# Attention beside linear attention on one core: part of the exponentials moved to VectorE, 32-row score tiles, and a listed order

## The chip, the cores and the metric

The kernel runs on one core of a Trainium2 chip. A core has TensorE (PE; its weight loads appear as PEld), ScalarE (ACT), VectorE (DVE), GpSimd (POOL) and SyncE (SP), which run side by side, each in its own program order, and wait for each other on semaphores. DMA queues move data between HBM and the on-chip memory SBUF. Matrix products land in PSUM, eight banks of 128 partitions x 512 fp32. The metric is the device time of one execution in microseconds (us), lower is better.

## The reference

Two attention blocks read the same `x` (2048 tokens, width 512, bf16), each with 32 heads of 16; a per-token gate mixes them.

```python
g = sigmoid((x * gate_w).sum(-1, keepdims=True))
# A: softmax attention
q, k, v = split_heads(x @ A_wqkv)                  # 32 heads of 16
p = softmax(q @ k.T * 16 ** -0.5)                  # 2048 x 2048 for each head
a = merge_heads(p @ v) @ A_wo
# B: linear attention
q, k, v = split_heads(x @ B_wqkv)
pq, pk = phi(q), phi(k)                            # phi(t) = t+1 if t>0 else exp(t), plus 1e-6
b = merge_heads((pq @ (pk.T @ v)) / (pq @ pk.sum() + 1e-6)) @ B_wo
out = g * a + (1 - g) * b
```

Block A needs 32 x 2048 x 2048 exponentials: 134 million, 1.05 million on each of the 128 partitions. A unit here is one head, 128 keys and 512 queries: a tile of 128 x 512 exponentials. There are 32 x 16 x 4 = 2048 units.

## The kernel before

Softmax is computed without subtracting a maximum; the row sum comes from a column of ones beside V, so one product gives numerator and denominator. The work goes in 32 rounds: four blocks `t8` of eight heads, two halves of four heads, four chunks `qc` of 512 queries. A round has 64 units (16 key blocks x 4 heads), cut into 22 groups (`sizes`, line 695: twenty of three units and two of two).

For each group the loop at the end of the function calls, in this order:

- `emit_ST` (line 710): one score matmul for each unit, 128 keys x 512 queries. A head has only 16 rows, but the stationary operand `KTpad` has all 128: `task_KPAD` (line 418) masks K with `maskK`, so that the seven other heads' rows are zeros. Group g writes banks 0 to 2 or 3 to 5 in turn (`b0 = 3 * (g % 2)`).
- `emit_EXP` (line 726): one ACT instruction over the whole group, 128 x 1536, from PSUM to `PT` in SBUF, which has four slots.
- `emit_PV` (line 734) of the group two before: `PT` is stationary in pieces of 128 x 128 and 32 columns of `Vaug` (16 of V, a one, 15 zeros) stream past it, four matmuls a unit, added up in bank 6 (`acc`).
- at a round's end `emit_round_end` (line 753): DVE takes the reciprocal of the row sums and scales the numerators.

Everything else is cut into steps with deadlines and costs (`enqueue`, `run_misc`): projections of Q, K, V, and block B. `run_misc` fits steps between groups by a credit of PE and DVE time, and none runs in the first two or last three groups of a round (`quiet`, line 926). All these steps share bank 7. Block B takes the exponential of phi from PSUM on ACT (`phi_ops`, line 513) and evicts the tile on DVE after it; `task_BQ` (line 582) takes reciprocals of whole 128 x 512 tiles of denominators in pieces of 128 columns. The first exponentials need a slice of `A_wqkv` (`wA0`), loaded on ACT's DMA queue behind two halves of `x` (`xnat`); the other halves of `x` come by DMA transposes on SP's queue.

Each engine's list is fixed when the program is built, and an engine that waits holds everything behind it. So ACT's step to the next group needs its banks filled, and PE can fill them only after ACT's instruction two groups before has ended.

Of the kernel before, what the change touches and what calls it, by code (L numbers as in the profile page):

```python
# [2 lines left out]

# [8 lines left out]
I32 = mybir.dt.int32  # L12


DEBUG_REQ = lambda env: []
STATS = {}
SCHED_LOG = []
# [18 lines left out]
class _Eng:  # L36
    def __init__(self, name, sem):
        self.name = name
        self.sem = sem
        self.ops = []  # L40
        self.n = 0
        self.inc_idx = []
        self.inc_val = []
        self.semval = 0
        self.waited = {}

# [9 lines left out]
    def add(self, fn, deps=(), inc=True, dma_sem=None):  # L56
        waits = []
        for d in deps:
            if d is None:
                continue  # L60
            if isinstance(d, _Raw):
                sem, val = d.sem, d.val
            else:
                sem, val = d.E.sem, d.E.cover(d.idx)
            key = id(sem)
            if val <= 0 or self.waited.get(key, 0) >= val:
                continue
            self.waited[key] = val
            for k, (s2, v2) in enumerate(waits):
                if s2 is sem:  # L70
                    if val > v2:
                        waits[k] = (sem, val)
                    break
            else:
                waits.append((sem, val))
# [10 lines left out]
class _Res:  # L86
    __slots__ = ("name", "w", "r")

    def __init__(self, name):
        self.name = name  # L90
        self.w = None
        self.r = {}

# [20 lines left out]

def bass_gated_mix__mha_block__linear_attn_block__prompt_kernel(
# [11 lines left out]
    assert Bsz == 1  # L127
    H = 32
    Dh = D // H
    assert Dh == 16 and D % 128 == 0 and S % 512 == 0  # L130
# [5 lines left out]
    NU = NTB * 4  # L136
    GS = 3
    NPT = 4

    with ExitStack() as es:  # L140
# [8 lines left out]

        xT = SB([128, NCC, S], BF16, "xT")  # L150
        NCP = NCC // 2
        xnat = SB([128, NTB, 128 * max(NCP, 1)], BF16, "xnat")
        dummy = SB([128, 2], FP32, "dummy")
        wA = SB([128, NCC, 3 * D], BF16, "wA")
        wA0 = SB([128, NCC, 3, 128], BF16, "wA0")
# [6 lines left out]
        pidx_i = SB([128, 1], I32, "pidxi")  # L162
        hidx_f = SB([128, 1], FP32, "hidxf")
        mtmp = SB([128, 8], FP32, "mtmp")
        maskK = SB([128, 8], FP32, "maskK")
        blockmask = SB([128, 128], BF16, "blockmask")
        KT = SB([128, 1, S], BF16, "KT")
        KTpad = SB([128, 2, 4, S], BF16, "KTpad")
        QT = SB([128, 2, NQC, 512], BF16, "QT")
        Vaug = SB([128, 2, NTB, 4, 32], BF16, "Vaug")  # L170
        PT = SB([128, NPT, 512 * GS], BF16, "PT")
        O_sb = SB([128, NTB, D], BF16, "Osb")
        rden = SB([128, 16], FP32, "rden")
        tpool = SB([128, 2, 512], FP32, "tpool")
        epool = SB([128, 2, 512], FP32, "epool")
        upool = SB([128, 2, 512], FP32, "upool")
        phiK = SB([128, 2, D], BF16, "phiK")
        vB = SB([128, 2, NCC, 136], BF16, "vB")
        kvacc = SB([128, NCC, 136], FP32, "kvacc")
        KVbd = SB([128, NCC, 128], BF16, "KVbd")  # L180
        Zexp = SB([128, NCC, 128], BF16, "Zexp")
        phiQT = SB([128, 2, NCC, 512], BF16, "phiQT")
        numT = SB([128, 2, 512], FP32, "numT")
        den = SB([128, 2, 512], FP32, "den")
        OBT = SB([128, 2, NCC, 512], BF16, "OBT")
        bB = SB([128, NQC, 4, D], BF16, "bB")
        OT = SB([128, 4, NCC, 128], BF16, "OT")
        NOUTT = 2
        outt = SB([128, NOUTT, D], BF16, "outt")
        eg = SB([128, NTB], FP32, "eg")  # L190
        gom = SB([128, 2, NTB], FP32, "gom")

        STATS["sbuf_free"] = nc.sbuf_bytes_remaining() if callable(getattr(nc, "sbuf_bytes_remaining", None)) else nc.sbuf_bytes_remaining
# [3 lines left out]
        spare = ps[:, 3584:4096]  # L197
        spare_bf = ps[:, 3584:4096].bitcast(BF16)
        acc4 = acc.rearrange("p (qb j c) -> p qb j c", qb=4, j=4)

        PE = _Eng("pe", SEM("s_pe"))
# [5 lines left out]
        semXN = [SEM("s_xn0"), SEM("s_xn1")]  # L207
        semW0 = SEM("s_w0")
# [3 lines left out]
        semW3 = SEM("s_w3")  # L212
        semOUT = [SEM(f"s_out{i}") for i in range(NOUTT)]
        out_counts = [0] * NOUTT

        R = _Res
        r_ring = [R(f"ring{b}") for b in range(6)]
        r_acc = R("acc")
        r_spare = R("spare")
        r_xT = [[R(f"xT{c}_{t}") for t in range(NQC)] for c in range(NCC)]  # L220
        r_xnat = [R(f"xnat{i}") for i in range(2)]
        r_wA = R("wA")
        r_wA0 = R("wA0")
        r_warm = R("warm")
        r_wB = R("wB")
        r_woA = R("woA")
        r_woB = R("woB")
        r_gw = R("gw")
        r_ident = R("ident")
        r_const = R("const")  # L230
        r_mask = R("mask")
        r_bmask = R("bmask")
        r_dummy = R("dummy")
        r_KT = [[R(f"KT{p}_{t}") for t in range(NQC)] for p in range(1)]
        r_KTpad = [[[R(f"KTpad{p}_{j}_{t}") for t in range(NQC)] for j in range(4)] for p in range(2)]
        r_QT = [[R(f"QT{p}_{q}") for q in range(NQC)] for p in range(2)]
        NVB = max(1, (NTB + 3) // 4)
        r_Vaug = [[R(f"Vaug{p}_{v}") for v in range(NVB)] for p in range(2)]
        r_Vaug_all = [r for row in r_Vaug for r in row]
        r_PT = [R(f"PT{i}") for i in range(NPT)]  # L240
        r_O = [R(f"O{qb}") for qb in range(NTB)]
        r_rden = R("rden")
        r_t = [R(f"t{i}") for i in range(2)]
        r_e = [R(f"e{i}") for i in range(2)]
        r_u = [R(f"u{i}") for i in range(2)]
        r_phiK = [R("phiK0"), R("phiK1")]
        r_vB = [R("vB0"), R("vB1")]
        r_kvacc = R("kvacc")
        r_KVbd = R("KVbd")
        r_Zexp = R("Zexp")  # L250
        r_phiQT = [[R(f"phiQT{p}_{i}") for i in range(NCC)] for p in range(2)]
        r_numT = [R("numT0"), R("numT1")]
        r_den = [R("den0"), R("den1")]
        r_OBT = [[R(f"OBT{p}_{i}") for i in range(NCC)] for p in range(2)]
        r_bB = [[R(f"bB{q}_{b}") for b in range(4)] for q in range(NQC)]
        r_OT = [R(f"OT{i}") for i in range(4)]
        r_outt = [R(f"outt{i}") for i in range(NOUTT)]
        r_eg = R("eg")
        r_g = R("g")

        def op(E, fn, reads=(), writes=(), inc=True, extra=()):
            deps = _deps_for(reads, writes) + list(extra)
            ev = E.add(fn, deps, inc=inc)
            _record(E, ev, reads, writes)
            return ev

# [8 lines left out]
        def dma(out_ap, in_ap, sem, reads=(), writes=(), total_after=None, noncontig=False, E=None, transpose=False):  # L275
            E = SP if E is None else E
            eng = {SP: nc.sync, AC: nc.scalar, PO: nc.gpsimd}[E] if E in (SP, AC, PO) else nc.sync
            deps = _deps_for(reads, writes)
            ev = E.add(lambda o=out_ap, i=in_ap, nz=noncontig, tr=transpose, eng=eng: _do_dma(eng, o, i, nz, tr),
                       deps, inc=False, dma_sem=sem)  # L280
            for res in reads:
                res.r[E] = _Raw(sem, total_after)
            for res in writes:
                res.w = _Raw(sem, total_after)
                res.r = {}
            return ev

        def pe_macro(fns, reads=(), writes=(), record=True, wait=True):
            assert fns
            deps = _deps_for(reads, writes) if wait else []  # L290
            first = None
            ev = None
            for k, fn in enumerate(fns):
                last = (k == len(fns) - 1)
                ev = PE.add(fn, deps if k == 0 else (), inc=(last and record))
                if k == 0:
                    first = ev
            if record:
                for res in reads:
                    res.r[PE] = first  # L300
                for res in writes:
                    res.w = ev
                    res.r = {}
            return ev

# [5 lines left out]

        x2 = A_x[0]
        out2 = out[0]
        wsrc = A_wqkv.rearrange("(cc p) n -> p cc n", p=128)
        if NCP > 0:
            for hh in range(2):
                dma(xnat[:, hh * (NTB // 2):(hh + 1) * (NTB // 2), :],
                    x2[hh * (S // 2):(hh + 1) * (S // 2), 128 * (NCC - NCP):D].rearrange("(tb p) c -> p tb c", p=128),
                    semXN[hh], writes=[r_xnat[hh]], total_after=16, E=AC)
        for k3 in range(3):  # L320
            dma(wA0[:, :, k3, :], wsrc[:, :, k3 * D:k3 * D + 128], semW0, writes=[], total_after=48, E=AC)
        r_wA0.w = _Raw(semW0, 48)
        dma(gw[:], gate_w.rearrange("(cc p) -> p cc", p=128), semG, writes=[r_gw], total_after=16, noncontig=True, E=AC)
        NCD = NCC - NCP
        for t in range(NQC):
            for cc in range(NCD):
                dma(xT[:, cc, 512 * t:512 * (t + 1)], x2[512 * t:512 * (t + 1), 128 * cc:128 * (cc + 1)], semXT[cc][t],
                    writes=[r_xT[cc][t]], total_after=16, transpose=True, E=SP)
        dma(wA[:], wsrc, semW1, writes=[r_wA], total_after=16)
        dma(wB[:], B_wqkv.rearrange("(cc p) n -> p cc n", p=128), semW2, writes=[r_wB], total_after=16)  # L330
        dma(woA[:], A_wo.rearrange("(i p) n -> p i n", p=128), semW3, writes=[r_woA], total_after=32)
# [710 lines left out]
```

## Time and profile before

| | |
|---|---|
| three runs, median (lowest to highest) | 972.21 us (972.05 to 972.5) |
| the profiled execution's own time: its span | 970.5 us |
| ACT busy | 945.0 us, 97% |
| PE busy | 832.4 us, 86% |
| DVE busy | 305.9 us, 32% |
| first group exponential starts / last one ends | 16.60 us / 961.9 us |
| group exponentials of 1536 and of 1024 columns | 640 and 64 |

The span runs from the first to the last instruction of the one execution that was profiled; the median is 1.7 us above it. Busy shares are averages, and a busy PE includes the pipelined ends of its matmuls. A row of the groups names the line, engine, operation and tiles, and then the busy time of all and the mean of one. Matmul rows have the line of a helper, so they are told apart by their tiles. The chain of waits follows the work that ended last back from the end of the program.

### The profile page before, as it was taken

To read this page: it belongs to the slowest core of one execution; us is meant where nothing else is said; L and a number is where in the kernel's file an instruction comes from. 1 tells how busy PE (TensorE), PEld (TensorE's weight loads), DVE (VectorE), ACT (ScalarE), POOL (GpSimd) and SP (SyncE) were. 2 spreads that over 40 slices of the span, in tenths; PEclk is the share of its full clock that TensorE was granted. 3 is DMA by queue.
4 is the path that set the end of the run, shared out by engine and by line. 5 is a ranking of instruction groups with operands and counts; after the bars stand their busy time and mean duration, and the time that the engine had idled before them with its cause. 6 is when DMAs were issued, how large, how long until landed. Compare 5 with 4: busy or idle time off the path is not lost.

```text
span 970.5 us, 25037 instructions
## 1 busy us (share of the span) xinstructions
PE 832.4 (86%) x11257; PEld 504.8 (52%) x11464; DVE 305.9 (32%) x591; ACT 945.0 (97%) x739; POOL 8.1 (1%) x42
## 2 busy tenths in 40 slices
PE   6988888898888988888888888888888898879886
PEld 3555555555555555555545555554555555545553
DVE  3311132032321223223654445344555431102112
ACT  3999999999999999999999999999999999999996
POOL 3000000000000000000000000000000000000000
PEclk8999999999999999999999999999999999999998
DMA  9000000000000000000000000000000000000001
GB/s 275 3 2 1 2 2 1 2 1 2 2 2 2 2 1 2 1 2 2 2 1 2 2 1 2 2 1 1 1 2 2 1 2 1 1 2 18 12 18 45
DMA packets 13067, 10.40 MB, mean 11 GB/s; under 512 B 6816, under 2 KB 11936, under 8 KB 12960
## 3 DMA queue, kind: packets, MB, share of 16 engines
q1 hardware_dynamic: 8768, 7.34, 2.5%
q10 hardware_dynamic: 4192, 1.44, 0.7%
q8 instruction: 90, 1.47, 0.6%
q14 instruction: 17, 0.14, 0.1%
HBM read 5.64 MB, written 2.10 MB: 8 GB/s over the span
## 4 chain that ended last, share of the span: by engine, by line
ACT 52%; PE 30%; issue 14%; DVE 2%; DMA 1%; ACTq 1%; DVEq 0%
ACT PT L730 51%; PE ps L307 30%; DVE den L613 1%; ACT epool L514 1%; DMA wA_5<-in_A_wqkv_dram 1%; DVE tpool L516 1%; ACTq L273 0%; DVE outt L677 0%; DVE den L607 0%; PE ps L310 0%; DMA out_dram<-outt 0%; DVE KTpad L425 0%; ACTq L992 0%; ACTq L985 0%; DVE KT L413 0%
## 5 line engine op out<-in xcount | busy, mean ns | idle before, releaser
L730 ACT ACTIVATE PT<-ps 128x1536 bf16<-128x1536 f32 (+1 forms) x704 | 934.2, 1465 | 10.6 <-PE ps L307 9.5
L307 PE MATMUL ps<-QT,KTpad 128*128 128x512 bf16 x1883 | 529.4, 381 | 116.6 <-ACT PT L730 108.4
L307 PEld LDWEIGHTS ps<-Vaug,PT 128*128 128x128 bf16 x8192 | 308.0, 96 | 166.7 <-ACT PT L730 0.8
L307 PE MATMUL ps<-Vaug,PT 128*128 128x32 bf16 x8192 | 313.8, 176 | 1.0 <-ACT PT L730 0.4
L307 PEld LDWEIGHTS ps<-QT,KTpad 128*128 128x128 bf16 x2048 | 152.4, 97 | 247.6 <-ACT PT L730 139.9
L756 DVE RECIPROCAL rden<-ps 128x16 f32<-128x16 f32 x32 | 8.2, 257 | 190.8 <-PE ps L307 190.8
L613 DVE RECIPROCAL den<-den 128x128 f32<-128x128 f32 x64 | 61.0, 953 | 2.2
L516 DVE COPY tpool<-ps 128x512 f32<-128x512 f32 x32 | 22.1, 691 | 91.0 <-ACT epool L514 91.0
L465 DVE CAST Vaug<-ps 128x256 bf16<-128x256 f32 x32 | 13.6, 424 | 78.9 <-PE ps L307 78.9
L425 DVE TENSOR_SCALAR KTpad<-KT,maskK 128x512 bf16<-128x512 bf16 x128 | 34.6, 346 | 0.1
L307 PE MATMUL ps<-wB,xT 128*128 128x512 bf16 x116 | 31.1, 377 | 3.1 <-DVE tpool L516 2.6
L564 DVE TENSOR_TENSOR kvacc<-ps,kvacc 128x258 f32<-128x258 f32 x32 | 13.7, 428 | 57.4 <-PE ps L307 57.4
L307 PE MATMUL ps<-xT,wA 128*128 128x512 bf16 x100 | 27.0, 377 | 0.5
L482 DVE CAST QT<-ps 128x512 bf16<-128x512 f32 x16 | 11.1, 691 | 42.4 <-PE ps L307 42.4
L413 DVE CAST KT<-ps 128x512 bf16<-128x512 f32 x16 | 11.1, 692 | 39.4 <-PE ps L307 39.4
L514 ACT ACTIVATE epool<-ps 128x512 f32<-128x512 f32 x32 | 21.8, 682 | 0.0
L677 DVE SCALAR_TENSOR_TENSOR outt<-ps,gom,bB 128x512 bf16<-128x512 f32 x16 | 11.8, 749 | 28.3 <-PE ps L307 26.8
L645 DVE TENSOR_SCALAR bB<-ps,gom 128x512 bf16<-128x512 f32 x16 | 12.0, 750 | 26.6 <-PE ps L307 26.6
L607 DVE TENSOR_SCALAR den<-ps 128x512 f32<-128x512 f32 x16 | 11.1, 691 | 29.6 <-PE ps L307 29.6
L307 PE MATMUL ps<-wA,xT 128*128 128x64 bf16 x448 | 18.7, 192 | 0.0
L307 PE MATMUL ps<-woA,OT 128*128 128x512 bf16 x58 | 16.6, 390 | 0.8 <-DVE OT L667 0.6
L667 DVE COPY OT<-ps 128x512 bf16<-128x512 bf16 (+2 forms) x20 | 7.1, 369 | 30.9 <-PE ps L310 30.9
(61 smaller groups left out, 246.1 us busy)
## 6 DMA issues: line engine op xcount, KB each, us to landing
out_dram<-outt SPq DMA_DIRECT2D x16, 128.0 KB, 1.7
wA<-in_A_wqkv_dram SPq DMA_DIRECT2D x1, 1536.0 KB, 7.0
wB<-in_B_wqkv_dram SPq DMA_DIRECT2D x1, 1536.0 KB, 10.3
xnat<-in_A_x_dram ACTq DMA_DIRECT2D x2, 512.0 KB, 5.3
woA<-in_A_wo_dram SPq DMA_DIRECT2D x1, 512.0 KB, 11.3
woB<-in_B_wo_dram SPq DMA_DIRECT2D x1, 512.0 KB, 12.2
wA_5<-in_A_wqkv_dram ACTq DMA_DIRECT2D x3, 128.0 KB, 6.9
xT<-in_A_x_dram SPq DMA_TRANSPOSE x8, 6.0
```

Of the source, the lines that this page charges most:

```text
L307: return lambda: nc.tensor.matmul(o, lhsT=l, rhs=r, start=start, stop=stop, skip_group_check=sg)
L413: op(DV, lambda par=par, t=t, sp_=sp_: nc.vector.tensor_copy(KT[:, par, 512 * t:512 * (t + 1)], sp_), reads=[rsp], writes=[r_KT[par][t]])
L425: op(DV, lambda hs=hs, j=j, t=t, par=par, half=half: nc.vector.tensor_scalar(KTpad[:, hs, j, 512 * t:512 * (t + 1)], KT[:, par, 512 * t:51 ...
L465: op(DV, lambda hs=hs, vb=vb, nb=nb, src=src: nc.vector.tensor_copy(Vaug[:, hs, vb:vb + nb, :, 0:16], src), reads=[rsp], writes=[r_Vaug[hs ...
L482: op(DV, lambda par=par, qc=qc, sp_=sp_: nc.vector.tensor_copy(QT[:, par, qc, :], sp_), reads=[rsp], writes=[r_QT[par][qc]])
L514: ev_e = op(AC, lambda e_s=e_s, sp_=sp_: nc.scalar.activation(epool[:, e_s, :], sp_, ACT.Exp), reads=[rsp], writes=[r_e[e_s]])
L516: op(DV, lambda e_s=e_s, sp_=sp_: nc.vector.tensor_copy(tpool[:, e_s, :], sp_), reads=[rsp], writes=[r_t[e_s]], extra=[ev_e])
L564: op(DV, lambda srcv=srcv, dstv=dstv: nc.vector.tensor_tensor(dstv, srcv, dstv, ALU.add), reads=[rsp, r_kvacc], writes=[r_kvacc])
L613: op(DV, lambda s=s, c4=c4: nc.vector.reciprocal(den[:, s, 128 * c4:128 * (c4 + 1)], den[:, s, 128 * c4:128 * (c4 + 1)]), reads=[r_den[s]] ...
L645: op(DV, lambda qc=qc, qbl=qbl, qb=qb, sp_=sp_: nc.vector.tensor_scalar(bB[:, qc, qbl, :], sp_, gom[:, 1, qb:qb + 1], None, op0=ALU.mult), ...
L677: op(DV, lambda s3=s3, qb=qb, qc=qc, qbl=qbl, sp_=sp_: nc.vector.scalar_tensor_tensor(out=outt[:, s3, :], in0=sp_, scalar=gom[:, 0, qb:qb ...
L730: op(AC, lambda slot=slot, b0=b0, n=n: nc.scalar.activation(PT[:, slot, 0:512 * n], ps[:, 512 * b0:512 * (b0 + n)], ACT.Exp, scale=SCALE), ...
```

## The change

The structure around the units is written anew; the tensors computed stay the same, and 1418 lines are added for 750 taken out.

- **A share of the exponentials goes to VectorE**, about a ninth of the units. Q is scaled so that the scores come out as 65536 times a base-2 exponent. DVE clamps a unit's scores from PSUM into int32 (`YI`). For three such units at a time it takes the low 16 bits as a fraction (two multiply-adds with a cubic's coefficients), shifts the high 16 bits into the exponent field of a bf16 (`E16`), and multiplies the two (`DP`). The constant term of the cubic is not added there: `E16` itself goes through a second set of products with `V2`, a copy of V scaled by that term. So a unit on VectorE has two sets of products with V. Only keys of blocks 12 to 15 can be taken.
- **Score tiles of 32 rows.** K and Q are no longer padded to 128 rows. A score matmul uses 32 partitions (two heads); `Qpad` has zeros in the other head's 16 rows. A group's three units lie on three different 32-row strips. `task_KPAD` is gone; four small DMAs on SP's queue fill `Qpad` for each chunk and half.
- **Zero products.** A product with V streams 64 columns, the unit's 32 and 32 zeros, instead of 32. `fill` adds matmuls by zeros into `acc` where the planner counts little PE work.
- **A listed order.** A planner with a time for each operation writes the engines' lists: units flow in groups of three across round ends (no groups of two), products wait in a list and are taken in the order in which they come ready, and DVE's work is ordered by priority. `PT` has six slots, `DP` three. Bank 7 is still the only one for projections, block B and the units that VectorE takes.
- **Block B**: DVE evicts first and ACT then reads SBUF; denominators are 8 columns per four heads instead of 128, one reciprocal of 128 x 128 for each chunk; results are transposed by DMA. The two output projections run in one PSUM group.
- **Start**: the first 512 tokens come in one DMA on ACT's queue, and the three `wA0` slices first on SP's queue. ACT makes three of the first evictions.
- **A check.** The largest and smallest reciprocal row sums are kept in `dev`. At the end they give a flag through one matmul and a maximum; PE, ACT, DVE and SP each wait for it, load it and branch. Behind the branch stands a general path that computes block A again with each row's maximum; it is run only if the flag is not zero.

```diff
+NTRI = 3
+KB2 = 12
...
-        KTpad = SB([128, 2, 4, S], BF16, "KTpad")
-        QT = SB([128, 2, NQC, 512], BF16, "QT")
+        Qs = SB([128, 2, 512], BF16, "Qs")
+        Qpad = SB([128, NQS, 512], BF16, "Qpad")
...
+        dma(xn0, x2[0:512, :].rearrange("(p tb) c -> p tb c", tb=4), semXN[0], writes=[r_xn0], total_after=16, E=AC,
+            lands=3.8)
+        op(PO, lambda: nc.gpsimd.memset(dummy[:], 0.0), writes=[r_dummy])
+        op(AC, lambda: nc.scalar.activation(dummy[:, 1:2], dummy[:, 0:1], ACT.Exp), reads=[r_dummy], writes=[r_dummy],
+           dur=1.6)
+        for k3 in (0, 1, 2):
+            dma(wA0[:, :, k3, :], wsrc[:, :, k3 * D:k3 * D + 128], semW0[k3], writes=[r_wA0[k3]], total_after=16, E=SP,
+                lands=4.5)
...
+        def unit_aps(r, u):
+            t8, qc, half = rounds[r]
+            kb, j = u // 4, u % 4
+            kt = KT[32 * j:32 * j + 32, t8 % 2, 128 * kb:128 * (kb + 1)]
+            q = Qpad[32 * j:32 * j + 32, r % NQS, :]
+            return kt, q, [r_KT[t8 % 2][kb // 4], r_Q[r % NQS]]
...
+        def pv_fns(r, u, p_ap, second, first):
...
+            v0 = V2[:, t8 % 2, kb - KB2, h, :] if second else Vaug[:, t8 % 2, kb, h, :]
+            own, zero_off = v0.offset, NV + NV2
+            for qb in range(4):
+                c = 128 * qb + 32 * j
+                if c + 64 <= 512:
+                    mv = bass.AP(tensor=v0.tensor, offset=own, ap=[list(v0.ap[0]), [zero_off - own, 2], [1, 32]])
+                    o = acc[:, c:c + 64]
...
+                fns.append(f_mm(o, p_ap[:, 128 * qb:128 * (qb + 1)], mv, start=(first and qb == 0), stop=False, sg=True))
...
+        def claim(r, u, b, beside):
...
+            pe_macro([f_mm(bank_ap(b), kt, q)], reads=rd, writes=[r_bank[b]], dur=(0.02 if beside else QK_T), mac=0.053, rows=32)
+            r_bank[b].tw = max(r_bank[b].tw, PE.t + 0.08)
+            push(1, [(lambda: nc.vector.tensor_scalar(YI[:, yi, 512 * k:512 * (k + 1)], bank_ap(b), Y_LO * FRAC, Y_HI * FRAC,
+                                                     op0=ALU.max, op1=ALU.min),
+                      [r_bank[b]], [r_YI[yi]], d_psum(512), None)])
...
+        def close_tri():
...
+            push(3, [
+                (lambda: nc.vector.scalar_tensor_tensor(out=pl, in0=lo, scalar=POLY_B, in1=lo, op0=ALU.add, op1=ALU.mult),
+                 [r_YI[yi]], [r_pol], d_sb(n), None),
+                (lambda: nc.vector.tensor_scalar(e16, hi, float(EXP_OFF + 127), 128.0, op0=ALU.add, op1=ALU.mult),
+                 [r_YI[yi]], [r_E16[dp]], d_sb(n, 0.5), None),
+                (lambda: nc.vector.scalar_tensor_tensor(out=w, in0=pl, scalar=POLY_C, in1=lo, op0=ALU.add, op1=ALU.mult),
+                 [r_YI[yi], r_pol], [r_DP[dp]], d_sb(n), None),
+                (lambda: nc.vector.tensor_tensor(w, w, eb, ALU.mult), [r_DP[dp], r_E16[dp]], [r_DP[dp]], d_sb(n, 0.5), None)])
+            for k, (r, u) in enumerate(us):
+                sl = slice(512 * k, 512 * (k + 1))
+                pv_pending.append((r, u, [(eb[:, sl], True), (w[:, sl], False)], r_DP[dp]))
...
+            op(AC, lambda slot=slot, b0=b0, n=n: nc.scalar.activation(
+                PT[:, slot, 0:n], ps[:, 512 * b0:512 * b0 + n], ACT.Exp, scale=LN2 / FRAC, bias=LN_KAPPA),
...
+        pe_macro([f_mm(bank_ap(tbank)[0:1, 0:128], vB[:, 0, 0, 0, 128:129], bad)], reads=[r_E16[0], r_vB[0][0]],
+                 writes=[r_bank[tbank]], dur=0.1)
+        op(DV, lambda: nc.vector.reduce_max(flag[0:1, 0:1], bank_ap(tbank)[0:1, 0:128], axis=AX.X), reads=[r_bank[tbank]],
+           writes=[r_flag], dur=0.3)
...
+            emit_ops(E, main[E], eng)
+            eng.wait_ge(flag_wait.sem, flag_wait.val)
+            v = eng.value_load(flag[0:1, 0:1])
+            with eng.If(v != 0):
+                emit_ops(E, general[E], eng)
```

## Prediction

> **What bounds the kernel now.** First the page's busy shares and its slices, for the engine that is full and when:
>
> ```profile
> PE 832.4 (86%) x11257; PEld 504.8 (52%) x11464; DVE 305.9 (32%) x591; ACT 945.0 (97%) x739; POOL 8.1 (1%) x42
> ...
> PE   6988888898888988888888888888888898879886
> ...
> DVE  3311132032321223223654445344555431102112
> ACT  3999999999999999999999999999999999999996
> ```
>
> ACT is full in every slice but the first and last; DVE is two thirds idle. Then the groups of instructions with their shapes kept apart:
>
> ```profile
> L730 ACT ACTIVATE PT<-ps 128x1536 bf16<-128x1536 f32 x640 | 875.7, 1500 | 10.6 <-PE ps L307 9.5
> L307 PE MATMUL ps<-QT,KTpad 128*128 128x512 bf16 x1883 | 529.4, 381 | 116.6 <-ACT PT L730 108.4 <-DVE QT L482 0.5 <-issue 0.2
> L730 ACT ACTIVATE PT<-ps 128x1024 bf16<-128x1024 f32 x64 | 65.5, 1114 | 0.0
> L613 DVE RECIPROCAL den<-den 128x128 f32<-128x128 f32 x64 | 61.0, 953 | 2.2
> L425 DVE TENSOR_SCALAR KTpad<-KT,maskK 128x512 bf16<-128x512 bf16 x128 | 34.6, 346 | 0.1
> L518 DVE TENSOR_SCALAR upool<-epool 128x512 f32<-128x512 f32 x32 | 13.3, 417 | 0.0
> L521 DVE SCALAR_TENSOR_TENSOR phiK<-tpool,upool 128x512 bf16<-128x512 f32 x16 | 11.1, 692 | 0.5
> L413 DVE CAST KT<-ps 128x512 bf16<-128x512 f32 x16 | 11.1, 692 | 39.4 <-PE ps L307 39.4
> ```
>
> The two forms of L730 hold 875.7 + 65.5 = 941 us of ACT; ACT sat idle for PE only 9.5 us, nearly all before its first, and PE 108 us for ACT. Now the timeline of a quiet stretch, for the pace (columns: start, length, engine, what):
>
> ```profile
> 499.87 0.82 PE L307 MATMUL ps<-QT,KTpad 128*128 128x512 bf16 x3 [0.23 <-ACT PT L730]
> 500.53 0.46 PE L307 MATMUL ps<-Vaug,PT 128*128 128x32 bf16 x12
> 501.21 0.82 PE L307 MATMUL ps<-QT,KTpad 128*128 128x512 bf16 x3 [0.23 <-ACT PT L730]
> ...
> 502.55 0.82 PE L307 MATMUL ps<-QT,KTpad 128*128 128x512 bf16 x3 [0.23 <-ACT PT L730]
> ```
>
> Each score triple is released by ACT, 1.34 us apart: that is ACT's step for 1536 columns (its 1.50 us rows overlap). Where steps are added PE sets the pace instead: at 946.76, 947.71, 949.52 score triples start 0.95 apart without and 1.81 apart with four output matmuls. So the chain of waits is of both:
>
> ```profile
> ACT 52%; PE 30%; issue 14%; DVE 2%; DMA 1%; ACTq 1%; DVEq 0%
> ```
>
> Last, the granted clock in windows near the end:
>
> ```profile
> 958.00:960.00 2.00, 1.40 (x27) 0.91 (x25) 0.00 (x0) 2.00 (x3) 0.00 (x0) 1.00 0.00 0
> ...
> 964.00:966.00 2.00, 1.49 (x3) 0.30 (x2) 1.41 (x2) 0.00 (x0) 0.00 (x0) 0.50 0.04 15
> ```
>
> Clock (third number from the right) stays 1.00 with PE busy 1.40 of 2 us, and is 0.50 after a thin stretch (0.67 of 2 us in 962 to 964).
>
> **The sum for before**, of the span of 970.5 us (1.7 below the median of the runs): head 16.6 to the first exponential; 640 x 1.34 = 857.6; 64 of 1024 columns at 1.34 - 0.43 (phi's 512 columns take 0.682, 1024 take 1.114) = 0.91, 58.2; 32 phi exponentials at 0.48 (307.33 to 307.81), 15.4; last end at 961.9, so 14.1 remain of 945.3, steps in which PE paced; tail 8.6.
>
> **ACT's work after.** A ninth of 2048 units is 228; 1820 remain, in groups of three across round ends: 607 x 1.34 = 813.4 in place of 915.8. Phi's 32 exponentials read SBUF instead of PSUM: no such row, between 0.43 (that difference) and the whole 0.68 of the row without overlap; 0.50, 16.0. The share itself is a count by the program; between a tenth (614 groups, +9) and an eighth (597, -13).
>
> **DVE.** It must hide all its new work behind ACT. For each claimed unit one clamp from PSUM, 512 columns, by the KT row 0.69: 228 x 0.69 = 157. For each of 76 triples: two multiply-adds of 1536, 0.692 (phi's row, 512 columns) + 1024 x 1.047 ns (0.424 for 256 and 0.692 for 512 in DVE's rows) = 1.76 each; one shift into the exponent and one product of two bf16. Those two have no row: at one column a cycle 1.76; at two, as row L518 runs (0.417 for 512, half of 1.047 a column), 0.95; I take 0.95, since both write 2-byte results in SBUF, nearest to L518's all-SBUF form. 76 x 5.42 = 412. Of the old 306 go the KTpad row (35), 57 of the denominators' reciprocals, 21 of their adds, copies and products, the bB and OT rows (22) and 4 of upool in bf16: 167 left, plus 12 for gate products, the check and evictions at the start. Together 748. Neighbours overlap by 0.076 (L425: 346 ns each, 34.6 us for 128); on half of some 880 instructions, 33: 715, 85% of 840 us of interior. It fits; with both unknown rows at 1.76 it is 838 and does not (rival 2). Bank 7 holds a claimed unit about 1.3 us (fill 0.38, two hand-overs, 0.69 out) and some 138 other steps 1.7: 296 + 235 = 531 of 840, and waits for a DVE busy with a 1.76 us instruction come on top. PE lists products of a claimed unit behind DVE: if they are late, everything behind them on PE, the next scores first, is late, and ACT stops two groups later.
>
> [...]
>
> **PE.** For each group of 1.34: score tiles. The trace has none of 32 rows; if the three run at once they cost one pass, 0.216 (the pitch of 512 columns: four output matmuls take 1.02 less a pipelined 0.377, over three), if in a row, 0.65 as now. I take one pass and three weight loads of 0.042 (12 take 0.56, one 0.096): 0.34, near the lower end, as the strips share no rows. Around them the shape of the array changes; unseen, from 0 to two emptied pipelines of 0.165 (0.381 - 0.216); I take one. Products with 64 columns: eight 64-column V matmuls take 0.39 with 0.19 each, pitch 0.0285, so 12 are 0.34 (now 0.31). Claimed units, 0.375 a group, with two sets of four products and a tile of 0.216: 0.17. Projections and block B: 512-column passes 64 for K, 64 for Q, 192 for block B, 128 for outputs, 448 x 0.216 = 97, plus V and small ones 25: 122/607 = 0.20. Sum 0.34 + 0.165 + 0.34 + 0.17 + 0.20 = 1.22 of 1.34. PE has 9% left where it has 0.95 of 1.34 in a quiet stretch now; the misc steps are spread over all groups instead of stopping at round ends. Zero fills go only into free time by the plan. At the far ends: 1.05 (no emptying) to 1.69 (in a row and both).
>
> The Trainium skill, TensorEngine Tiling (Array Packing), section Key Properties, says that changing the tiling mode drains TensorE, and that speaks against a design that changes it twice for every group; by it the PE sum would be 1.38, over ACT's 1.34, or 607 x 0.04 = 24 us more. The page TensorE: Matmul & The Clock Gate, section Measured speedup vs the span model, gives four row strips 3.07 times the pace of one, an estimate of 0.28 for four tiles, below my 0.34. The trace has neither.
>
> **ACT's waits in the interior** are 14.1 now. The new list has less slack on both PE and DVE; but group-sized jams (four matmuls at once, 1.81) become pieces of two. I take 15; from 5 to 55 (5% of the interior, if lateness of DVE products comes through on one group in ten by half a microsecond, 30, and the opening rounds lose as much as the head saves).
>
> **Head.** Now the slice `wA0` lands at 11.18, after five starts on ACT's queue, and 5.4 us later the first exponential runs. The slices start first on SP instead: at 1.15 us each (3.44 for three) and 7 to land, K's is in by about 9, then projections, an eviction and scores as now less V's share: 12.3, between 10 and 15. The masks of K disappear (1.14). Moved behind: the DMA transposes of `x`, needed only from key block 4 on, that is six groups later.
>
> **Tail.** Now 8.6: round end, transposes, one matmul, an eviction, then two stores that wait 1.19 us for buffers. The waiting goes (four buffers), about -2. The flag's path (a comparison, a matmul, a maximum) runs beside the stores; then four engines load a word and branch, which no row shows: 0 to 6, 2 taken. 8.6 again. The Trainium skill, Runtime: NRT & Kernel Launch, Instruction fetch mechanics, says that a taken branch outside the fetched pages stalls for a fetch; the branch over the general path is one. No figure there.
>
> Sum: 12.3 + 813.4 + 16.0 + 15.0 + 8.6 = 865.3 of span, plus 1.7 as now: **867 us**.
>
> **The rivals.** (1) PE becomes the pace: with both emptied pipelines 1.38, and pieces that cannot be fitted, 1.38 to 1.48 a group: 607 x 1.38 = 838 + 16 + 15 + 21 + 1.7 = 892, up to 952 (1.48). For it: only 9% slack. Against: the rows of strips overlap.
> (2) DVE becomes the pace: 838 of work, head and tail 21, gaps of 5%, and 1.7: about 903. For it: neither 2-byte form is in the trace. Against: the planner stops claiming when DVE has 4 us in hand, so lateness makes fewer claims only if its own times are right.
> (3) Fewer waits and an eighth claimed: 867 - 13 - 8 = 846.
> (4) The other side: the clock. A 32-row tile occupies a quarter of the rows; if the clock gate counts that, the grant falls, as it does at 0.67 of 2 us busy. All of PE's 1.22 scales. It decides when 1.22/clock passes (970.5 - 37)/607 = 1.54 a group, at a mean grant of 0.79; at 0.75: 607 x 1.63 + 39 = 1026. For it: the trace's own falls to 0.50. Against: PE's busy share stays near 0.8, and doubled product columns and fills feed it.
> That VectorE does not relieve ACT at all is excluded by the count of units.
>
> **How the numbers follow.** Forecast 0.60; rival 1 0.12; rival 2 0.09; rival 3 0.09; rival 4 0.08; the rest, 0.02, within 0.2% (970 to 974; 0.2% is what these runs, spread over 0.05%, can tell with a comparison's own noise) or just above. The forecast's own range is 852 to 885. To leave out no more than 2 in 10 the range reaches down to the eighth, 846 less 2, and up over rival 2 and the lower half of rival 1, to 1.42 a group: 844 to 915. Faster 0.90, same 0.01, slower 0.09.
>
> **What would show it.** Right: about 607 exponentials of 1536 at a pitch of 1.34 and none of 1024 but the last; 228 clamps of 0.69; the two unknown DVE rows near 0.95; DVE busy near 715; score triples that start within a weight load of each other; clock 1.00 in the interior; first exponential near 12.3. Wrong: ACT's idle time for PE over 50 us (rival 1 or 2: who is named before PE tells which), DVE above 93% with a shift row of 1.76, slices with a clock below 0.9, or far fewer claimed units.

## The result

The changed kernel takes 866.23 us (median; 864.01 to 869.25) against 972.21 us: a ratio of 0.8911, 95% interval 0.8892 to 0.8929. The forecast was 867, range 844 to 915, so sign, size and range held. The profiled execution has a span of 862.3 us and a time of 864.01, 1.7 us around the span as before.

The page of the changed kernel, busy shares and slices:

```profile
PE 759.0 (88%) x12259; PEld 437.9 (51%) x12259; DVE 686.1 (80%) x877; ACT 838.5 (97%) x648; POOL 9.4 (1%) x20
...
PE   8988899898888988988889989998888888889995
...
DVE  4599993979999996389999999658999998794142
ACT  5999999999999999999999999999999999999994
```

ACT is still the full engine, and shorter by 106 us; DVE, idle for two thirds before, is now 90% busy or more in 24 of its 40 slices. The groups with shapes kept apart:

```profile
L1451 ACT ACTIVATE PT<-ps 128x1536 bf16<-128x1536 f32 x607 | 831.1, 1863 | 4.9 <-PE ps L519 4.8
L519 PE MATMUL ps<-Vaug,PT 128*128 128x64 bf16 x7292 | 301.1, 194 | 0.5 <-DVE Osb L1021 0.5
L1138 DVE TENSOR_SCALAR YI<-ps 128x512 int32<-128x512 f32 x225 | 154.4, 686 | 37.7 <-PE ps L519 35.9
L1156 DVE SCALAR_TENSOR_TENSOR pol<-YI 128x1536 f32<-128x1536 uint16 x75 | 131.8, 1757 | 2.1
L1160 DVE SCALAR_TENSOR_TENSOR DP<-pol,YI 128x1536 bf16<-128x1536 f32 x75 | 131.2, 1749 | 0.0
L1158 DVE TENSOR_SCALAR E<-YI 128x1536 int16<-128x1536 int16 x75 | 71.3, 951 | 0.0
L1162 DVE TENSOR_TENSOR DP<-DP,E 128x1536 bf16<-128x1536 bf16 x75 | 71.1, 948 | 0.0
L1451 ACT ACTIVATE PT<-ps 128x1024 bf16<-128x1024 f32 x1 | 1.3, 1299 | 0.0
```

225 units went to VectorE, 75 triples, and ACT kept 607 groups of 1536 columns and one of 1024. Both 2-byte rows that the trace of before could not show take 0.951 and 0.948 us for 1536 columns, two columns in the time of one beside the multiply-adds' 1.75. ACT was idle 4.9 us before its group exponentials, 4.8 of it for PE. A stretch of the timeline (start, length, engine, what):

```profile
403.23 0.61 PE L519 MATMUL ps<-xT,wB 128*128 128x512 bf16 x2
403.26 1.22 ACT L779 ACTIVATE epool<-tpool 128x512 bf16<-128x512 f32 x1
403.67 0.51 PE L519 MATMUL ps<-Vaug,PT 128*128 128x64 bf16 x12
403.78 3.39 ACT L1451 ACTIVATE PT<-ps 128x1536 bf16<-128x1536 f32 x2
404.12 0.39 PE L519 MATMUL ps<-Qpad,KT 32*128 32x512 bf16 x3
404.44 0.52 PE L519 MATMUL ps<-Vaug,PT 128*128 128x64 bf16 x12
```

Three score tiles take 0.39 us together, as long as one of them; the products behind them start 0.32 after (0.65 before). The twelfth product before them began at 403.67 + 0.51 - 0.194 = 403.99, so the scores start 0.13 after it where products follow each other by 0.029: 0.10 us more, put down here to the change of the tiles' shape (experiment e5 below has no such change and no such gap). Phi's exponential moves ACT on by 0.52 (403.26 to 403.78).

Last, the granted clock. In windows of 4 us it is below 0.99 in four places of the interior of the changed kernel, in none of the kernel before. One of them (the clock is the third number from the right):

```profile
408.00:412.00 4.00, 3.45 (x62) 1.89 (x58) 3.08 (x5) 4.00 (x4) 0.00 (x0) 1.00 0.01 4
412.00:416.00 4.00, 2.91 (x42) 1.92 (x40) 3.23 (x8) 4.00 (x4) 0.00 (x0) 0.67 0.00 0
416.00:420.00 4.00, 4.00 (x80) 2.84 (x77) 3.91 (x5) 3.81 (x3) 0.00 (x0) 0.91 0.02 4
```

The loss is 4 x 0.33 + 4 x 0.09 = 1.7 us of clock, or 3.4 us at half; a finer window, 413.40 to 416.70, has 0.50 throughout. The clock record of this trace has four such drops before the last exponential ends, at 413.3, 464.5, 672.8 and 747.9, each 3.41 us long and at half. Just before this one, from 411.76 to 413.66, PE had only two score triples to do.

### The profile page after: what moved, and what is told of

Read it like the earlier page. It is cut to its first block, busy times and chain, and to the rows that moved or that the text cites. A ratio compares the mean times of both kernels' runs of the same rounds, so it can differ in the third digit from the quotient of the medians.

```text
span 862.3 us, 27178 instructions
## 1 busy us (share of the span) xinstructions
PE 759.0 (88%) x12259; PEld 437.9 (51%) x12259; DVE 686.1 (80%) x877; ACT 838.5 (97%) x648; POOL 9.4 (1%) x20
## 3 DMA queue, kind: packets, MB, share of 16 engines
q10 hardware_dynamic: 2016, 1.57, 0.7%
## 4 chain that ended last, share of the span: by engine, by line
ACT 58%; PE 20%; issue 17%; DVE 4%; ACTq 0%; POOL 0%; DVEq 0%; POOLq 0%
ACT PT L1451 56%; PE ps L519 20%; ACT epool L779 3%; DVE pol L1156 1%; PE ps L522 0%; DVE YI L1138 0%; DVE E L1158 0%; DVE DP L1160 0%; DVE tpool L782 0%; DVE Vaug L736 0%; DVE KT L681 0%; DVE Osb L1021 0%; DVE pol L1529 0%; DVE xT L1382 0%; DVE phi L785 0%
## 5 line engine op out<-in xcount | busy, mean ns | idle before, releaser
L1451 ACT ACTIVATE PT<-ps 128x1536 bf16<-128x1536 f32 x608 | 832.0, 1862 | 4.9 <-PE ps L519 4.8
L519 PE MATMUL ps<-Qpad,KT 32*128 32x512 bf16 x2048 | 288.0, 386 | 84.7 <-ACT PT L1451 71.2
L519 PE MATMUL ps<-Vaug,PT 128*128 128x64 bf16 x7292 | 301.1, 194 | 0.5 <-DVE Osb L1021 0.5
L519 PEld LDWEIGHTS ps<-Vaug,PT 128*128 128x128 bf16 x7292 | 245.7, 98 | 104.6 <-issue 96.3
L519 PEld LDWEIGHTS ps<-Qpad,KT 32*128 32x128 bf16 x2048 | 72.9, 91 | 226.0 <-ACT PT L1451 195.4
L1138 DVE TENSOR_SCALAR YI<-ps 128x512 int32<-128x512 f32 x225 | 154.4, 686 | 37.7 <-PE ps L519 35.9
L1156 DVE SCALAR_TENSOR_TENSOR pol<-YI 128x1536 f32<-128x1536 uint16 x75 | 131.8, 1757 | 2.1
L1160 DVE SCALAR_TENSOR_TENSOR DP<-pol,YI 128x1536 bf16<-128x1536 f32 x75 | 131.2, 1749 | 0.0
L1158 DVE TENSOR_SCALAR E<-YI 128x1536 int16<-128x1536 int16 x75 | 71.3, 951 | 0.0
L1162 DVE TENSOR_TENSOR DP<-DP,E 128x1536 bf16<-128x1536 bf16 x75 | 71.1, 948 | 0.0
```

The costliest lines, as they stand in the source:

```text
L519: return lambda: nc.tensor.matmul(o, lhsT=l, rhs=r, start=start, stop=stop, skip_group_check=sg)
L1138: push(1, [(lambda: nc.vector.tensor_scalar(YI[:, yi, 512 * k:512 * (k + 1)], bank_ap(b), Y_LO * FRAC, Y_HI * FRAC, op0=ALU.max, op1=ALU.min),
L1156: (lambda: nc.vector.scalar_tensor_tensor(out=pl, in0=lo, scalar=POLY_B, in1=lo, op0=ALU.add, op1=ALU.mult), [r_YI[yi]], [r_pol], d_sb(n), ...
L1158: (lambda: nc.vector.tensor_scalar(e16, hi, float(EXP_OFF + 127), 128.0, op0=ALU.add, op1=ALU.mult), [r_YI[yi]], [r_E16[dp]], d_sb(n, 0.5) ...
L1160: (lambda: nc.vector.scalar_tensor_tensor(out=w, in0=pl, scalar=POLY_C, in1=lo, op0=ALU.add, op1=ALU.mult), [r_YI[yi], r_pol], [r_DP[dp]], ...
L1162: (lambda: nc.vector.tensor_tensor(w, w, eb, ALU.mult), [r_DP[dp], r_E16[dp]], [r_DP[dp]], d_sb(n, 0.5), None)])
```

## The experiments

All are edits of the changed kernel, numbered e1 to e12 in the text. Times are medians; the kernel before took 972.2 to 972.6 beside them.

**What VectorE's share is worth.** One function returns early, and the planner gives every unit to ACT (e1):

```diff
         def can_claim(now, js):
 
-            r = claim_round()
-            if r is None:
-                return None
-            t8, qc, half = rounds[r]
+            return None
             if (t8, qc, half) not in q_done or (t8, 3) not in k_ready:
                 return None
```

> The changed kernel with VectorE taking no unit: all 2048 go to ScalarE in 683 groups of three, by the same planner. Theory (the time is the number of group exponentials at one pitch): 683 x 1.34 = 915 + 17 for phi + a head of 10.9 + waits of 3 + a tail of 13 + 1.7 = 960 us, 94 above the changed kernel. Rival (a good part of the gain is the new order, the narrow tiles and the shorter start, and VectorE's share only moves work about): below 930 us.

Measured 962.92 us (ratio to before 0.990, 0.9886 to 0.9919), clock 0.988 to 0.992. ACT's row on the page:

```profile
L1448 ACT ACTIVATE PT<-ps 128x1536 bf16<-128x1536 f32 (+1 forms) x683 | 931.9, 1921 | 3.8 <-PE ps L519 3.6
```

The count of groups at one pitch gives 75 x 1.34 = 100.5 us between this and the changed kernel; measured are 962.92 - 866.23 = 96.7. So of the 106 us gained nine tenths are VectorE's, and all the rest of the rewriting together is 9.3 us.

**Whether the clock follows busy time or the share of the array in use.** First the zero columns taken out, lists otherwise the same (e2):

```diff
-                    mv = bass.AP(tensor=v0.tensor, offset=own, ap=[list(v0.ap[0]), [zero_off - own, 2], [1, 32]])
-                    o = acc[:, c:c + 64]
+                    mv = bass.AP(tensor=v0.tensor, offset=own, ap=[list(v0.ap[0]), [1, 32]])
+                    o = acc[:, c:c + 32]
...
```

> The changed kernel with 32-column products with V, the 32 zero columns taken out of each, and the same lists otherwise. Theory (the granted clock follows how much of the array works, and the zero columns hold it up): the clock falls in many stretches, a mean grant of 0.75 to 0.92, and the time goes to 885 to 1000 us. Rival (the clock follows only whether PE is busy): mean grant 0.98 to 0.99 and 864 to 869 us.

Measured 885.94 us (0.9112, 0.9093 to 0.913), mean clock 0.815. Then the fills, taken out with their time kept free (e3):

```diff
-            pe_macro([f_mm(acc, warm[:, 0:128], warm[:, 0:512], start=False, stop=False, sg=True)], reads=[r_warm],
-                     writes=[r_acc], dur=MM512, mac=0.216)
+            mac_log.append((PE.t, 0.216))
+            PE.t += MM512
```

> The changed kernel without the 100 filling matmuls by zeros, their time kept free in the list. Theory (the clock follows how much of the array works): more drops of 3.4 us than the changed kernel's four, mean grant 0.93 to 0.98, 868 to 885 us. Rival (fills do nothing, as PE waits for ScalarE anyway): 864 to 869 us with the same few drops.

Measured 883.01 us (876.3 to 884.16; 0.9083, 0.9068 to 0.9098), clock 0.927 to 0.94; its trace has 22 drops where the changed kernel has four. Both agree with the theory and not with the rival: with less of the array at work PE's busy share is nearly as high as before (88% and 86%, for 88%), and the clock falls. A part of that busy time is only matmuls made longer by the low clock, so the share alone proves little here; e4 and e5 below settle it. The page of the narrow products, busy shares and clock slices:

```profile
PE 775.1 (88%) x12137; PEld 414.8 (47%) x12259; DVE 687.2 (78%) x877; ACT 845.5 (96%) x648; POOL 9.4 (1%) x20
...
PEclk9897679896878878997876587799768555879998
```

**What the strips are worth.** All score tiles on one strip (e4):

```diff
-            kt = KT[32 * j:32 * j + 32, t8 % 2, 128 * kb:128 * (kb + 1)]
-            q = Qpad[32 * j:32 * j + 32, r % NQS, :]
+            kt = KT[0:32, t8 % 2, 128 * kb:128 * (kb + 1)]
+            q = Qpad[0:32, r % NQS, :]
```

> The changed kernel with every score tile on the first 32-row strip, so that no two can run side by side; the lists are the same instruction by instruction. It computes all scores from the heads of the first strip. Theory (the strips run at once, and PE has little to spare): a score triple takes 0.65 in place of 0.32 us, PE's work for a group goes from about 1.14 to 1.47 to 1.57 us, and the time to 930 to 1000 us. Rival (PE's slack or the spread steps hide it): below 885 us.

Measured 1685.7 us (one run): 1.7 times the theory's upper bound, so both readings missed the price. The page and the timeline say why:

```profile
PE 1638.2 (97%) x12137; PEld 754.5 (45%) x12259; DVE 705.2 (42%) x877; ACT 900.2 (53%) x648; POOL 9.4 (1%) x20
...
PEclk9555555555675555555555555558955555555555
```

```profile
800.90 1.46 PE L519 MATMUL ps<-Qpad,KT 32*128 32x512 bf16 x3
802.29 0.82 PE L519 MATMUL ps<-Vaug,PT 128*128 128x64 bf16 x12
```

PE is 97% busy and gets 0.545 of its clock. A triple takes 1.46 us, three tiles in a row at half speed, and everything else on PE is slow with it. A quarter of the rows in use for most of the time does not hold the clock, however busy PE is. This mixed two things; the next run parts them, with the whole array for each score tile (e5):

```diff
-            kt = KT[32 * j:32 * j + 32, t8 % 2, 128 * kb:128 * (kb + 1)]
-            q = Qpad[32 * j:32 * j + 32, r % NQS, :]
+            kt = KT[:, t8 % 2, 128 * kb:128 * (kb + 1)]
+            q = Qpad[:, r % NQS, :]
```

> The changed kernel with score tiles of all 128 rows, so that they run one after the other with the whole array in use; the lists are the same. Each score is then the sum of four heads' scores. It parts the two things that the one-strip kernel mixed, tiles in a row and the clock. Theory (in a row costs 0.33 us a group, the clock stays up): a score triple 0.65, no emptying at mode changes (0.10 saved), PE's work 1.36 to 1.45 us a group, granted clock 0.99 or more without any drop, and 880 to 925 us. Rival (the narrow tiles matter only through the clock): below 872 us.

Measured 902.7 us (0.9283, 0.9266 to 0.93), clock 0.998:

```profile
PE 877.9 (97%) x12259; PEld 548.9 (61%) x12259; DVE 689.3 (77%) x877; ACT 858.5 (95%) x648; POOL 9.4 (1%) x20
...
PEclk9999999999999999999999999999999999999999
...
PE 77%; ACT 9%; DVE 8%; issue 5%; POOL 0%; ACTq 0%; DVEq 0%; POOLq 0%
```

```profile
400.26 0.81 PE L519 MATMUL ps<-Qpad,KT 128*128 128x512 bf16 x3
400.91 0.51 PE L519 MATMUL ps<-Vaug,PT 128*128 128x64 bf16 x12
```

The products start 0.65 us after a triple's first tile, for 0.32 with strips. Scores that follow products without waiting start 0.03 after the last of them here (median of the trace), for 0.13 in the changed kernel. In the chain of waits PE is now the pace. 902.7 less 1.7 and some 40 of head, tail and phi over 608 groups is an estimate of 1.42 us of PE a group; with strips, 0.33 less for the triple and 0.10 more for the change of shape, it is 1.19. So the strips are what keeps PE under ACT's 1.34, and they are worth 36 us here. At equal busy share, 97%, the clock is 0.998 with all rows and 0.545 with a quarter: this is the plainest evidence that the grant follows the part of the array in use. The changes of shape are not what lowers it: the changed kernel has as many of them as the one-strip kernel, and holds 0.98 to 0.99.

**Whether DVE has room.** The shift is issued twice, 0.95 us more for each triple, and the planner does not count it (`dur` 0; e6):

```diff
+                (lambda: nc.vector.tensor_scalar(e16, hi, float(EXP_OFF + 127), 128.0, op0=ALU.add, op1=ALU.mult),
+                 [r_YI[yi]], [r_E16[dp]], 0.0, None),
                 (lambda: nc.vector.tensor_scalar(e16, hi, float(EXP_OFF + 127), 128.0, op0=ALU.add, op1=ALU.mult),
```

> The changed kernel with the shift into the exponent done twice for each triple, 0.95 us more of VectorE each and 72 us in all, unknown to the planner: DVE at the load that the forecast's upper bound for this row would have given. Theory (VectorE has room): DVE busy near 755 us, 866 to 875 us. Rival (VectorE's lists are tight, and products that come late hold up PE and the scores behind them): 885 us or more.

Measured 941.0 us (935.38 to 944.12; 0.9688, 0.9662 to 0.9713). The theory fell: 72 us more on an engine that was 80% busy came out as 75 us more time. (The list is not quite the old one: with the extra instruction the planner claimed 228 units, 76 triples, in place of 225.) The page's shares, the chain, and the waits (engine, line, what it waited for, us, times, longest):

```profile
PE 804.0 (86%) x12270; PEld 460.5 (49%) x12270; DVE 761.5 (82%) x960; ACT 850.5 (91%) x647; POOL 9.4 (1%) x20
...
DVE 48%; PE 33%; issue 12%; ACT 7%; POOL 0%; ACTq 0%; DVEq 0%; POOLq 0%
```

```profile
ACT PT L1453 <- PE ps L519: 62.6, 102, 2.0
PE ps L519 <- DVE YI L1138: 55.0, 86, 2.0
...
PE ps L519 <- DVE Osb L1021: 18.1, 18, 3.0
```

ACT waits for PE, and PE for DVE to empty bank 7 of a claimed unit's scores (YI) or `acc` (Osb), with the next group's scores listed behind. While PE waits the clock falls too, to 0.905 to 0.919; what part of the 75 us that makes was not parted. The same with the true time in the planner (e9):

```diff
-                 [r_YI[yi]], [r_E16[dp]], 0.0, None),
+                 [r_YI[yi]], [r_E16[dp]], d_sb(n, 0.5), None),
```

> The shift done twice as in e6, but with its true time of 0.95 us in the planner, which then claims 213 units in place of 225 and writes 612 groups. Theory (e6's 75 us came from a list written with a wrong time: products and evictions listed on PE before DVE has them, and the scores behind them): 868 to 880 us, four groups at 1.34 and a little over. Rival (DVE has no room for 72 us more, whatever the list): 915 us or more.

Measured 871.71 us (0.8956, 0.8942 to 0.897), with 612 groups. The page:

```profile
PE 768.3 (88%) x12221; PEld 440.7 (51%) x12221; DVE 719.9 (83%) x920; ACT 845.3 (97%) x652; POOL 9.4 (1%) x20
```

The row still costs twice as much, but the list knows it and takes 71 triples in place of 76: 4 to 5.5 us remain (against 867.7 in this batch, or 866.23), about what four more groups at 1.34 make. So nearly all of the 75 us are gone once the list is written with the true time. That the list alone does it is not shown: DVE has 42 us less to do here than in e6 (720 for 762), and a list with 76 triples and the right times was not run.

**The end.** Without the wait, load and branch, and the general path behind it (e7):

```diff
-            eng.wait_ge(flag_wait.sem, flag_wait.val)
-            v = eng.value_load(flag[0:1, 0:1])
-            with eng.If(v != 0):
-                emit_ops(E, general[E], eng)
+            if E is SP:
+                eng.wait_ge(flag_wait.sem, flag_wait.val)
```

> The changed kernel without the wait for the flag, its load and the branch on the four engines, and without the general path; the flag itself is still computed, and SP waits for it. Theory (the 3 us between the landing of the last store and the end of the span are the load and the branch): 2.5 to 4 us less, 862 to 864 us. Rival (that time is the end of any program, or the flag's late arrival): within 0.5 us of the changed kernel.

Measured 862.58 us (861.23 to 864.83; 0.8871, 0.8857 to 0.8885), 3.7 less than the first 866.23. The last instruction of DVE, the maximum for the flag, ends 5.05 us before the span's end in the changed kernel and 2.0 us before it here: 3.0 us are the wait, load and branch together. Then a false order taken out (e10):

```diff
         r_outl = [R(f"outl{k}") for k in range(4)]
+        for x in r_outl:
+            x.w, x.r = r_pol.w, dict(r_pol.r)
...
-            w = [r_outl[k], r_pol]
+            w = [r_outl[k]]
```

> The changed kernel with one false order taken out of its end: the four last output tiles all name the same scratch tensor as written, so that DVE's two evictions wait for ACT's two; here each names only its own quarter. Theory (DVE's last evictions start 1.7 us late, and the stores behind them end the span): 1.2 to 2 us less, 864 to 865 us. Rival (ACT's stores or the flag end the span): no change within 0.5 us.

Measured 866.18 us (0.891, 0.8895 to 0.8924) beside 867.7 for the unchanged one: the difference of 1.5 is within the intervals, so the times alone leave it open. In the two traces DVE's last evictions end 3.6 us after the first of the last output matmuls in the changed kernel (853.44 to 857.07) and 2.1 after it here (856.96 to 859.10), and the span ends 8.86 and 7.44 after it.

**More fills.** `MAC_LOW` from 0.45 to 0.60 gives 217 fills (e8):

> The changed kernel with the planner's floor for array work raised from 0.45 to 0.60, which gives 217 filling matmuls in place of 100 and the same 608 groups. Theory (each drop of the clock costs about 1 us or more, and fills prevent drops): mean grant above 0.992, and 860 to 864 us. Rival (the fills take PE time that the scores need): 868 us or more.

Measured 868.37 us (0.8931, 0.8916 to 0.8945), clock 0.976 to 0.985. The theory fell: the clock is no higher, and six drops stand in this trace where the changed kernel had four, mostly at other places. The rival isn't shown either: its 868 is met, but the unchanged kernel's 866.23 and 867.7 lie within this one's runs (865.82 to 870.59). The planner places fills by its own times, and on the chip thin stretches arise elsewhere. Why these are left was not settled.

**A version that beats both.** As e10, with more claims from each round (e11):

```diff
-        MIN_LEFT, MIN_LEFT_LAST = 38, 30
+        MIN_LEFT, MIN_LEFT_LAST = 22, 16
```

> As e10, and VectorE may claim from a round until 22 units are left in place of 38; the planner then claims 234 units and writes 605 groups in place of 608. Theory (groups count): 3 x 1.34 = 4 us less than e10, 859 to 862 us. Rival (DVE at 80% is already what its list can bear): as e10 or more.

Measured 860.43 us (859.53 to 862.91; 0.8854, 0.8841 to 0.8866). 234 units, 605 groups. It is 7.3 us under the unchanged kernel of the same chip, whose interval it doesn't touch, and 5.8 under e10, where three groups explain 4.0. The unchanged kernel (e12):

> The changed kernel again, unchanged, beside these three on the same chip: 864 to 869 us, with the runs of lower mean clock the longer ones.

Measured 867.7 us (0.8922, 0.891 to 0.8934). Its runs have mean clocks of 0.986 to 0.977 and times of 865.4 to 868.68. With the first four (0.989 and 864.01, 0.978 and 869.25 at the ends), 0.011 of mean clock goes with 5.2 us, that is some five or six drops of 3.4 us at half, an estimate of about 1 us each. The two traces of this kernel give 0.7: four times 3.4 us at half with a span of 862.3, six times with 863.7. So the spread of this kernel, 0.6% where the one before had 0.05%, goes with the clock that was lost; which is the cause was not tested.

## Why the prediction was right

The terms of the sum against the profiled span of 862.3 us (865.3 forecast). The first group starts at 10.86, the last ends at 849.35.

| term | forecast | measured |
|---|---|---|
| head | 12.3 | 10.9 |
| group exponentials at 1.34 | 813.4 (607) | 814.3 (607 and one short, at the same 1.34) |
| phi's exponentials | 16.0 | 16.6 (32 x 0.52) |
| waits in the interior | 15.0 | 7.6 (what is left of 838.5) |
| tail | 8.6 | 12.95 |

Only the count of the second row is measured. In the trace 467 of the 574 steps between full groups that have no phi between them are 1.33 us; the forecast's 1.34 holds some waiting already. At 1.33 the groups take 808.2 and 13.7 are left as waits, near the forecast's 15. By the same sums the kernel before had 14.1 of waits at 1.34, and 20.5 at 1.33.

**The bound and the count** were right, and they carry the result: e1 shows 96.7 us for 75 groups, 1.29 each.

**DVE's rows** were right: 0.69 for a clamp, 1.76 and 1.75 for the multiply-adds, 0.95 for the two unknown ones. They add up to 686 us in all, not 715: the new work is 9 us less (225 units, not 228), the rest 7 less, and neighbours overlap by 45 us where 33 were taken. The Trainium skill, VectorE: DVE Perf Modes, section What auto-detection actually checks, asks for step 1 only where 2-byte values are packed in pairs; for one source with source and result in SBUF it has a second two-per-cycle mode without that condition, and the row that reads with step 2 agrees, at 0.951. What these two rows cost matters through the list. Rival 2 set 903 us on both at 1.76; with one of them at 1.90 (e6, e9) the time is 941 with a list that does not know it and 872 with one that does. The step that was wrong is that DVE's new work fits as long as its sum is below ACT's interior: e6's 762 us of some 840 fit by that sum, and cost 75. In fixed lists work is hidden only if it comes when the list says so. The prediction names this lateness, but prices it in its waits at 55 us at most.

**PE's sum** of 1.22 was close, 1.19 by the estimate from e5: triple 0.32 for 0.34, change of shape 0.10 for 0.165, products 0.029 as taken. The drain at mode changes that the Trainium skill names, TensorEngine Tiling (Array Packing), section Key Properties, agrees with the 0.10 us, a gap that e5 doesn't have; it was too small to lift PE over ACT. Rival 1 is what e5 makes: 902.7 at 1.42 a group, where the rival's sum gives 607 x 1.42 + 54 = 916.

**The clock**, rival 4, was the right fear and mispriced, and the sign "clock 1.00 in the interior" did not hold: there are the four drops. The clock does follow the part of the array in use, and without the zero columns (e2) or the fills (e3) it falls. The Trainium skill, TensorE: Matmul & The Clock Gate, section What's actually happening, lets the gate follow how busy PE has been; e4 and e5, both 97% busy with 0.545 and 0.998, show that busy time alone does not set it. The rival scaled all of PE's work by the mean clock: at 0.815 that is 1.50 a group and some 950 us, while e2 took 886. One part of this is that 32-column products are shorter (0.025 for 0.029); another may be that drops begin in stretches with little for PE to do, where PE has time to lose; the two were not parted. Where the load itself cannot hold the clock, as in e4, the whole price comes: the 1.47 to 1.57 a group expected there, over 0.545, is 2.7 to 2.9, and (1685.7 - 40)/608 is 2.7.

**The tail** was mis-sized by 4.4 us. The flag's load and branch took 3.0 where 2 were taken, the false order some 1.4, and PE has seven output matmuls of a later tile listed in front of the last products (849.44 to 850.09, some 0.6); the rest of the 4.4 was not traced. **The head** was 1.4 shorter, and the waits 7.4 fewer (at 1.34 a group): ACT waited less than before, not more (whether the smaller pieces of the steps did that was not tested). These errors cancelled to 3 us; that 867 came so near to 866 is luck, as the sum was better than its parts.

## What to carry to other kernels

When the full engine runs one kind of instruction at one pitch, count those instructions first: here 915.8 us of group exponentials became 814.3, and that difference alone, taken from 972.2, gives 871, within 1% of the result. In lists written ahead, a second engine's load is nearly free only at the times that the list assumes; before trusting a busy share of 80%, ask who waits behind each of its results, and measure each operation's time rather than bound it. When tiles are cut to a part of the array, look at the granted clock, not at PE's busy share.

## What the runs showed of the hardware

- The granted clock averaged 0.545 with PE 97% busy on 32-row tiles of one strip, and 0.998 with PE 97% busy on 128-row tiles. Moving columns of zeros helped to hold it: products of 64 columns, half of them zeros, had 0.98 to 0.99, of 32 columns 0.815.
- One drop lasts 3.4 us at half (four of 3.41 us in the changed kernel's trace).
- Three tiles of 32 rows on three strips take as long as one (0.39 us), and the next matmul may start 0.32 after; scores behind products of another shape started 0.10 us later than without a change of shape (0.13 for 0.03).
- A shift of int16 read with step 2 took 0.951 us for 1536 columns and a product of two bf16 0.948, against 1.75 to 1.76 for multiply-adds.
- Waiting for a word, loading it and branching on four engines over a path not taken cost 3.0 us at the end.
